# Merging two DMA transposes, moving four more chunks' transposes from PE to DMA, and splitting the last copy out of PSUM

## The chip, the cores and the metric

The kernel runs on one core of a Trainium2 chip. The core has five engines with an instruction stream each: PE (TensorE, matrix multiplication; its weight loads are shown as PEld), DVE (VectorE), ACT (ScalarE), POOL (GpSimd) and SP (SyncE, which here issues nearly all DMAs). Transfers run on 16 DMA engines beside them. The metric is the time of one execution in microseconds; the median of the runs of the kernel before is 185.22 us.

## What is computed

Two layers in a row, for 4 batches, 8 heads, 768 steps and a head size of 48. The first is a gated linear attention with a state per head, the second an MLP with a squared ReLU (the code calls it MoE) over 3072 tokens, with 384 inputs and 2048 hidden units:

```python
for t in range(S):
    state = alpha[:, :, t, :, None] * state + einsum('bhd,bhe->bhde', k[:, :, t], v[:, :, t])
    y[:, :, t] = einsum('bhd,bhde->bhe', q[:, :, t], state)
x = y.transpose(0, 2, 1, 3).reshape(B * S, H * D)
h = x @ w_in
out = (maximum(h, 0) ** 2) @ w_out
```

All inputs and the output are float32 in memory; the kernel multiplies in bf16.

## The kernel before

**Tiling.** Attention runs in chunks of 128 steps. There are 24 (variable `s`, 0 to 23), six for each of the four batches, and a chunk of attention makes exactly one tile of 128 tokens for the MLP. For a chunk, ACT takes the logarithm of alpha, PE sums it up over the steps with a triangular matrix, and ACT takes the exponential of the sums and of their negatives. q is multiplied by the one and k by the other on DVE. Their product over the head size (the PSUM tile `sc`) is masked on DVE (`sm`, line 566) and multiplied by v; the contribution of the state is added; ACT copies the result to bf16 (`xn`, line 615, through the helper of line 388).

**q and k with the head size on the partitions.** The product `sc` needs q and k transposed. For chunks below `RAW = 11`, PE transposes them after the multiplication. From chunk 11 on ("raw"), POOL casts q and k to bf16 (`rawb`, line 415) and SP issues a DMA transpose for each of them (line 418) from `rawb` into `rawt`. DVE then multiplies the transposed q (line 509) and k (`kz`, line 513, two instructions) by exponentials that were computed transposed. `rawb` and `rawt` have three buffers (`NR = 3`), so a cast waits for the transpose three chunks back, and a transpose for the multiplications three chunks back.

**x with the features on the partitions.** The MLP needs `xn` transposed as well (`xT_big`). For most chunks PE does it with three matmuls against an identity (`tr`, line 243), and DVE copies the result out of PSUM (line 633, recorded as line 390). For the chunks of `XTURN = (18, 23)`, that is 18 to 22, SP issues a DMA transpose instead (line 625).

**The MLP** runs over groups of token tiles, mostly pairs. The first matmul of a pair is 48 matmuls of 256 columns; ACT applies the ReLU (line 681), DVE squares (line 689); the second matmul is 16 matmuls of 384 columns a tile. A tile's result is copied from PSUM by ACT or DVE (lines 727 and 729) and stored by a DMA. A chunk's share of the two is about 5.1 us of PE.

**The order.** All instructions of an engine stand in an order that is fixed when the program is built. A planner (class `Plan`) makes it: it gives each operation an assumed duration and latency, goes through time, and on each engine picks the operation that can start first. A DMA transpose stands on the planner's own queue `TR`. It is taken to occupy the DMA engines for its duration, to be done at its start plus duration plus latency (`TLD` and `TLAT`), and to be issued `late` microseconds after it could be (`TLATE`), which moves it back in SP's list. PE is given a slack of 0.25 us behind other engines' results. On the chip nothing of these times remains, only the order: each engine runs its list and waits where an input is not there. SP runs its list in the same way, so an issue that waits holds the ones behind it.

**The gate.** A chunk's first matmul may be planned only when the MLP has come far enough. With `prog` the MLP work already picked, in microseconds:

```python
return s <= LEAD + (prog["m1"] + prog["m2"]) / 5.12
```

`LEAD` is 3.5, so attention runs at most 3.5 chunks ahead of the MLP's mean progress.

**The end.** From 163.7 us on only MLP work is left. The last tile's second matmul ends at 181.33 us; one ACT copy of 128x384, the DMA of the output and the program's closing follow.

Of the kernel before, what the change touches and what calls it, by code (L numbers as in the profile page):

```python
# [8 lines left out]
FP32 = mybir.dt.float32  # L9
# [45 lines left out]
def after(op, x=0.0):  # L55
    return (op, x)
# [85 lines left out]
def kernel(  # L142
# [10 lines left out]
    nc = tc.nc  # L153
    B, H, S, D = q.shape
    HD = H * D
    P = 128
# [3 lines left out]
    d_model, d_ff = moe_w_in.shape  # L160
# [3 lines left out]
    NT = n_tok // P  # L164
# [13 lines left out]
    opool = ctx.enter_context(tc.tile_pool(name="opool", bufs=6))  # L178
# [15 lines left out]
        out=utri_f, in_=utri_f, compare_op=ALU.is_ge, fill=0.0,  # L194
# [41 lines left out]
    def pin(ins):  # L236
        tc.keep_in_program_order(ins)
# [19 lines left out]
    X_SLACK = 0.2  # L257
    LD = 0.98
    LD1 = 1.0
    WLD = 2.1  # L260
    LAG = 3.2
    SQ_PRIO = 0.0

    def add(eng, dur, emit, *deps, **kw):
        return plan.add(Op(eng, dur, emit, deps, **kw))
# [41 lines left out]
    C = [dict() for _ in range(NT)]  # L307
# [58 lines left out]
    def add_load(s, nm):  # L366
        d = C[s]
        b, c = divmod(s, NCH)

        def ld():  # L370
            if nm not in d:
                d[nm] = loads.tile([P, H, D], FP32, name=nm)
            pin(nc.sync.dma_start(out=d[nm], in_=SRC[nm][b, c]))
        prev = C[s - LB].get("use_" + nm) if s >= LB else None
        d["ld_" + nm] = add("DMA", LD if s < 4 else LD1, ld, prev, lat=2.0 if s < 4 else LAG if s < 6 else 2.4, at=0.6)

    def add_chunk(s):
        d = C[s]
        b, c = divmod(s, NCH)
# [3 lines left out]
        g = dict(prio=-10.0 + s * 0.01)  # L383
# [26 lines left out]
        if raw:  # L410
            w, wz = s % NR, s % 2

            def e_rb(j, nm):
                raw_tiles()
                pin(nc.gpsimd.tensor_copy(R["b"][:, w, j, :, 0:D], d[nm]))  # L415

            def e_turn(j):
                pin(nc.sync.dma_start_transpose(out=R["t"][:, w, j], in_=R["b"][:, w, j].rearrange("p h d -> p (h d)")))
            rt = []
            for j, nm in enumerate(["qt", "kt"]):  # L420
                cb = add("POOL", 0.55, lambda j=j, nm=nm: e_rb(j, nm), d["ld_" + nm],
                         *([C[s - NR]["turn"][j]] if s >= RAW + NR else []), prio=-5.0)
# [57 lines left out]
        if raw:  # L480
# [8 lines left out]
            aT = add("ACT", 0.48, e_AT, pT, after(ai) if ai else None, **g)  # L489
            aiT = add("ACT", 0.48, e_AiT, pT, after(aT), *([C[s - 2]["p2"]] if s >= RAW + 2 else []), **g)  # L490
# [20 lines left out]
        def e_kz(hh):  # L511
            rows = slice(DP * hh, DP * hh + DP)
            pin(nc.vector.tensor_mul(R["z"][rows, wz, :, hh, :], R["t"][rows, w, 1], R["i"][rows, wz]))  # L513
        if raw:
            if not last:
                mk = d["use_kt"] = add("DVE", 0.47, e_kI, ai, d["ld_kt"], old, **g)
            cp = add("DVE", 0.34, e_qAT, aT, rt[0], **g)
            prz = C[s - 2]["p2"] if s >= RAW + 2 else None
            kz0 = add("DVE", 0.45, lambda: e_kz(0), aiT, rt[1], prz, **g)
            kz1 = add("DVE", 0.45, lambda: e_kz(1), aiT, rt[1], prz, after(kz0), **g)  # L520
# [50 lines left out]
        if not last:  # L571
# [7 lines left out]
            prev = C[s - 1].get("sb") if s else None  # L579
# [116 lines left out]
    def add_moe2(g, tt, before, box, quarters, pools):  # L696
# [22 lines left out]
        def e_ev():  # L719
# [7 lines left out]
                pin(nc.vector.tensor_copy(box["ob"], box["po"]))  # L727
            else:
                pin(nc.scalar.copy(box["ob"], box["po"]))  # L729
        ev = add({"DVE": 0.47, "ACT": 0.38}, 0, e_ev, op, prio=-15.0)  # L730
        box["first"].gives = ev

        def e_held():
# [11 lines left out]
        if pool_out:  # L745
            o = add("POOL", 1.0, e_out, ev, prio=5.0)
            o.late, o.moves = 0.5, 0.5
        else:
            add("OUT", 0.55, e_out, ev, at=0.0).late = OUT_LATE
        return op  # L750

    DMA_ORDER = ["at", (0, "qt"), (0, "kt"), (1, "qt"), (1, "kt"), (0, "vt"), (2, "qt"),
# [117 lines left out]
```

## Time and profile before

| | |
|---|---|
| median of 3 runs | 185.22 us (184.88 to 185.26) |
| the profiled execution | 186.47 us |
| its span, first to last instruction | 184.7 us |
| PE busy | 177.7 us (96%) |
| DVE, ACT, POOL busy | 130.6, 126.7, 41.8 us |
| matmuls for transposing `xn` (line 243) | 57, in 19 chunks |
| DMA transposes of q and k (line 418) | 26, landing after 2.6 / 3.3 / 5.2 us (min / median / max) |
| DMA transposes of `xn` (line 625) | 5, landing after 2.3 / 3.5 / 4.9 us |

The page gives the busy time of each engine, the same in 40 slices of the span (one digit is tenths), and the chain of work that ended last, followed back from the end. A row of a timeline has the start in us, the duration, engine, line, operation, written tile <- read tiles, and a count; brackets hold the idle time before it and what ended it. "SPq" is an issue by SP; "landing" is the time from an issue to its data's arrival. A DMA's issue on SP can contain a wait. Matmuls overlap: one with 256 columns is recorded as 272 ns, but they follow each other every 109 ns.

### The profile page before, as it was taken

To read this page: it belongs to the slowest core of one execution; us is meant where nothing else is said; L and a number is where in the kernel's file an instruction comes from. 1 tells how busy PE (TensorE), PEld (TensorE's weight loads), DVE (VectorE), ACT (ScalarE), POOL (GpSimd) and SP (SyncE) were. 2 spreads that over 40 slices of the span, in tenths; PEclk is the share of its full clock that TensorE was granted. 3 is DMA by queue.
4 is the path that set the end of the run, shared out by engine and by line. 5 is a ranking of instruction groups with operands and counts; after the bars stand their busy time and mean duration, and the time that the engine had idled before them with its cause. 6 is when DMAs were issued, how large, how long until landed. Compare 5 with 4: busy or idle time off the path is not lost.

```text
span 184.7 us, 4919 instructions
## 1 busy us (share of the span) xinstructions
PE 177.7 (96%) x1886; PEld 133.5 (72%) x1886; DVE 130.6 (71%) x283; ACT 126.7 (69%) x288; POOL 41.8 (23%) x81
## 2 busy tenths in 40 slices
PE   7798999999999999999999999999999999999992
PEld 2467795467868887977867867868876877978661
DVE  1248898965899998776878877868866786845100
ACT  3657699606867996958958958958965975848221
POOL 8121100011161134142224242243243311000000
PEclk9969999999999999999999999999999999999999
DMA  5999999999989888989999899999999967601112
GB/s 167 215 216 243 270 367 331 324 233 214 209 169 218 171 173 165 177 155 172 154 168 205 158 196 177 237 186 155 220 164 205 207 97 248 202 4 43 41 47 85
DMA packets 120056, 34.12 MB, mean 185 GB/s; under 512 B 112384, under 2 KB 118784, under 8 KB 120032
## 3 DMA queue, kind: packets, MB, share of 16 engines
q1 hardware_dynamic: 119392, 31.83, 83.6%
q0 software_dynamic: 640, 1.97, 3.1%
q8 instruction: 15, 0.25, 0.6%
q14 instruction: 9, 0.07, 0.2%
HBM read 25.17 MB, written 4.72 MB: 162 GB/s over the span
## 4 chain that ended last, share of the span: by engine, by line
PE 88%; ACT 6%; DMA 2%; issue 1%; DVE 1%; SPq 0%; ACTq 0%
PE bank L240 76%; PE sc L240 5%; PE bank L243 5%; ACT r L681 3%; DMA at<-in_alpha_dram 2%; PE st L240 2%; DVE w_out_b L295 1%; ACT A L464 0%; ACT gT L343 0%; ACT xn L388 0%; ACT Ainv L468 0%; ACT w_in_b L297 0%; ACT qkT L388 0%; ACT L_s L398 0%; ACT ob L729 0%
## 5 line engine op out<-in xcount | busy, mean ns | idle before, releaser
L240 PE MATMUL bank<-xT_big,w_in_b 128*128 128x256 bf16 (+2 forms) x636 | 73.6, 262 | 0.1
L240 PE MATMUL bank<-w_out_b,gT 128*128 128x384 bf16 x384 | 71.1, 326 | 0.5 <-DVE w_out_b L295 0.5
L681 ACT ACTIVATE r<-bank 128x512 bf16<-128x512 f32 x96 | 55.9, 618 | 7.3 <-PE bank L240 6.2
L240 PEld LDWEIGHTS <-w_in_b 128*128 128x128 bf16 x636 | 53.3, 98 | 8.0 <-issue 0.2
L240 PEld LDWEIGHTS <-gT 128*128 128x128 bf16 x400 | 36.0, 98 | 20.1 <-DVE w_out_b L295 1.0
L689 DVE TENSOR_TENSOR gT<-r 128x512 bf16<-128x512 bf16 x96 | 40.9, 455 | 9.6 <-ACT r L681 8.8
L566 DVE TENSOR_TENSOR sm<-sc,utri_b 128x512 bf16<-128x512 f32 x48 | 30.8, 684 | 5.9 <-PE sc L240 5.7
L407 POOL CAST vb<-vt 128x384 bf16<-128x384 f32 x24 | 13.5, 561 | 65.6 <-DMA vt<-in_v_dram 52.2
L729 ACT COPY ob<-bank 128x384 f32<-128x384 f32 x16 | 7.7, 478 | 19.1 <-PE bank L240 18.8
L507 DVE TENSOR_TENSOR kI_s<-kt,Ainv 128x384 bf16<-128x384 f32 x21 | 12.4, 591 | 7.3 <-ACT Ainv L468 7.3
L388 ACT CAST xn<-bank 128x384 bf16<-128x384 f32 x24 | 11.5, 479 | 8.3 <-PE bank L240 8.3
L415 POOL CAST rawb<-qt 128x384 bf16<-128x384 f32 x13 | 8.0, 614 | 19.8 <-DMA qt<-in_q_dram 15.7
L591 ACT CAST sb<-st 128x384 bf16<-128x384 f32 x20 | 9.7, 484 | 3.8 <-DVE st L586 3.6
L586 DVE TENSOR_TENSOR st<-st,ae_s 128x384 f32<-128x384 f32 x20 | 11.2, 559 | 1.5 <-ACT ob L729 0.5
L513 DVE TENSOR_TENSOR kz<-rawt,kz 64x512 bf16<-64x512 bf16 x26 | 11.5, 441 | 1.1 <-ACT kz L456 0.4
L415 POOL CAST rawb<-kt 128x384 bf16<-128x384 f32 x13 | 7.9, 607 | 17.7 <-DMA kt<-in_k_dram 16.5
L240 PE MATMUL bank<-warm 128*128 128x256 bf16 (+1 forms) x48 | 10.5, 356 | 1.3 <-DVE warm L188 1.3
L504 DVE TENSOR_TENSOR qA_s<-qt,A 128x384 bf16<-128x384 f32 x11 | 6.1, 551 | 7.7 <-ACT A L464 7.7
L398 ACT ACTIVATE L_s<-at 128x384 bf16<-128x384 f32 x20 | 10.6, 530 | 0.2
L468 ACT ACTIVATE Ainv<-bank 128x384 bf16<-128x384 f32 x21 | 10.6, 503 | 0.0
L240 PEld LDWEIGHTS <-qkT 64*128 64x128 bf16 (+1 forms) x168 | 7.9, 96 | 3.1 <-issue 0.8
L240 PEld LDWEIGHTS <-sm 128*128 128x128 bf16 x192 | 8.2, 96 | 1.5 <-DVE sm L566 0.2
(65 smaller groups left out, 181.4 us busy)
## 6 DMA issues: line engine op xcount, KB each, us to landing
qt<-in_q_dram SPq DMA_DIRECT2D x24, 192.0 KB, 4.1
kt<-in_k_dram SPq DMA_DIRECT2D x24, 192.0 KB, 3.7
vt<-in_v_dram SPq DMA_DIRECT2D x24, 192.0 KB, 3.8
at<-in_alpha_dram SPq DMA_DIRECT2D x20, 192.0 KB, 3.9
wo<-in_moe_w_out_dram SPq DMA_DIRECT2D x4, 768.0 KB, 8.3
out_dram<-ob POOLq DMA_DIRECT2D x10, 192.0 KB, 3.6
wi<-in_moe_w_in_dram SPq DMA_DIRECT2D x4, 384.0 KB, 5.4
wi<-in_moe_w_in_dram SPq DMA_DIRECT2D x2, 768.0 KB, 7.9
```

What stands on the lines that cost most here:

```text
L240: pin(nc.tensor.matmul(*a, **kw))
L388: pin(nc.scalar.copy(out_t, in_t))
L398: pin(nc.scalar.activation(L[:, :, 0:D], d["at"], AF.Ln))
L407: pin(nc.gpsimd.tensor_copy(d["vb"], d["vt"]))
L415: pin(nc.gpsimd.tensor_copy(R["b"][:, w, j, :, 0:D], d[nm]))
L468: pin(nc.scalar.activation(d["Ai"], d["pm"][:, 0:HD].rearrange("p (h d) -> p h d", h=H), AF.Exp, scale=-1.0))
L507: pin(nc.vector.tensor_mul(kI[:, :, 0:D], d["kt"], d["Ai"]))
L513: pin(nc.vector.tensor_mul(R["z"][rows, wz, :, hh, :], R["t"][rows, w, 1], R["i"][rows, wz]))
L566: pin(nc.vector.tensor_mul(d["sm"][:, hh], d["sc"][:, hh], utri_b.to_broadcast([P, NP, P])))
L586: pin(nc.vector.tensor_mul(st4, st4, bcast(ae, D)))
L681: pin(nc.scalar.activation(box["r"][:, 0:w], box["ph"][:, 0:w], AF.Relu))
L689: pin(nc.vector.tensor_mul(gT[g][:, f0:f0 + per, lo * P:lo * P + n], r, r))
```

## The change

Three edits and the planner's numbers that go with them.

1. For raw chunks, q and k of a chunk, which lie side by side in `rawb`, go through one DMA transpose of 128 x 1024 instead of two of 128 x 512. It waits for both casts. Both multiplications on DVE, and the cast three chunks later, now depend on that one transpose. The planner assumes 1.2 + 4.5 us with `late` 1.5 (before 1.0 + 4.0 and 2.0 for each of the two), and 0.93 instead of 1.0 us for each load from chunk 11 on.
2. `XTURN` becomes (14, 23): `xn` of chunks 14 to 17 is transposed by DMA too. The planner takes 0.6 + 9.5 us for it (`XLAT`; before 0.8 + 4.0) and issues it 0.2 instead of 1.0 us late. The gate lets attention lead by more: 0.25 chunk more for each chunk from 12 on, up to 1.25 from chunk 16 on.
3. The last token tile is copied from PSUM by DVE (columns 0 to 191) and ACT (192 to 383); the planner may start both together, and the output's DMA waits for both.

```diff
+    LD2 = 0.93
...
-    XTURN = (18, 23)
-    TLD, TLAT, TLATE = 1.0, 4.0, 2.0
+    XTURN, XLAT = (14, 23), 9.5
+    TLD, TLAT, TLATE = 1.2, 4.5, 1.5
...
-        d["ld_" + nm] = add("DMA", LD if s < 4 else LD1, ld, prev, lat=2.0 if s < 4 else LAG if s < 6 else 2.4, at=0.6)
+        d["ld_" + nm] = add("DMA", LD if s < 4 else LD1 if s < RAW else LD2, ld, prev, lat=2.0 if s < 4 else LAG if s < 6 else 2.4, at=0.6)
...
-            def e_turn(j):
-                pin(nc.sync.dma_start_transpose(out=R["t"][:, w, j], in_=R["b"][:, w, j].rearrange("p h d -> p (h d)")))
+            def e_turn():
+                pin(nc.sync.dma_start_transpose(
+                    out=R["t"][:, w].rearrange("p j n t -> p (j n) t"), in_=R["b"][:, w].rearrange("p j h d -> p (j h d)")))
...
-                t_ = add("TR", TLD, lambda j=j: e_turn(j), cb, *([C[s - NR]["turned"][j]] if s >= RAW + NR else []), lat=TLAT)
-                t_.late = TLATE
-                rt.append(t_)
-            d["turn"] = rt
+                rt.append(cb)
+            d["turn"] = turn = add("TR", TLD, e_turn, *rt, *(C[s - NR]["turned"] if s >= RAW + NR else []), lat=TLAT)
+            turn.late = TLATE
...
-            d["x"] = add("TR", 0.8, e_xt, xn, lat=TLAT)
-            d["x"].late = 1.0
+            d["x"] = add("TR", 0.6, e_xt, xn, lat=XLAT)
+            d["x"].late = 0.2
...
+        def e_half(eng, lo, hi):
+            if eng == "DVE":
+                box["ob"] = opool.tile([P, d_model], FP32, name="ob")
+                pin(nc.vector.tensor_copy(box["ob"][:, lo:hi], box["po"][:, lo:hi]))
+            else:
+                pin(nc.scalar.copy(box["ob"][:, lo:hi], box["po"][:, lo:hi]))
+        half = None
+        if t == NT - 1:
+            half = add("DVE", 0.26, lambda: e_half("DVE", 0, d_model // 2), op, prio=-15.0)
+            ev = add("ACT", 0.22, lambda: e_half("ACT", d_model // 2, d_model), op, after(half, -9.0), prio=-15.0)
+        else:
+            ev = add({"DVE": 0.47, "ACT": 0.38}, 0, e_ev, op, prio=-15.0)
...
-            return s <= LEAD + (prog["m1"] + prog["m2"]) / 5.12
+            return s <= LEAD + min(1.25, max(0.0, 0.25 * (s - 11))) + (prog["m1"] + prog["m2"]) / 5.12
```

More of the change, by code (lines that the diff above doesn't have):

```diff
@@ L421, in add_chunk @@
                 cb = add("POOL", 0.55, lambda j=j, nm=nm: e_rb(j, nm), d["ld_" + nm],
-                         *([C[s - NR]["turn"][j]] if s >= RAW + NR else []), prio=-5.0)
+                         C[s - NR]["turn"] if s >= RAW + NR else None, prio=-5.0)
                 d["use_" + nm] = cb
-                t_ = add("TR", TLD, lambda j=j: e_turn(j), cb, *([C[s - NR]["turned"][j]] if s >= RAW + NR else []), lat=TLAT)
-                t_.late = TLATE
-                rt.append(t_)
-            d["turn"] = rt
+                rt.append(cb)
+            d["turn"] = turn = add("TR", TLD, e_turn, *rt, *(C[s - NR]["turned"] if s >= RAW + NR else []), lat=TLAT)
+            turn.late = TLATE
         vb = d["use_vt"] = add("POOL", 0.55, e_vb, d["ld_vt"], old, prio=-5.0)
@@ L516, in add_chunk @@
                 mk = d["use_kt"] = add("DVE", 0.47, e_kI, ai, d["ld_kt"], old, **g)
-            cp = add("DVE", 0.34, e_qAT, aT, rt[0], **g)
+            cp = add("DVE", 0.34, e_qAT, aT, turn, **g)
             prz = C[s - 2]["p2"] if s >= RAW + 2 else None
-            kz0 = add("DVE", 0.45, lambda: e_kz(0), aiT, rt[1], prz, **g)
-            kz1 = add("DVE", 0.45, lambda: e_kz(1), aiT, rt[1], prz, after(kz0), **g)
+            kz0 = add("DVE", 0.45, lambda: e_kz(0), aiT, turn, prz, **g)
+            kz1 = add("DVE", 0.45, lambda: e_kz(1), aiT, turn, prz, after(kz0), **g)
             d["turned"] = [cp, kz1]
@@ L729, in e_ev @@
                 pin(nc.scalar.copy(box["ob"], box["po"]))
-        ev = add({"DVE": 0.47, "ACT": 0.38}, 0, e_ev, op, prio=-15.0)
+        def e_half(eng, lo, hi):
[10 more added lines that the diff above has]
+            ev = add({"DVE": 0.47, "ACT": 0.38}, 0, e_ev, op, prio=-15.0)
         box["first"].gives = ev
@@ L748, in add_moe2 @@
         else:
-            add("OUT", 0.55, e_out, ev, at=0.0).late = OUT_LATE
+            add("OUT", 0.55, e_out, ev, half, at=0.0).late = OUT_LATE
         return op
```

## The prediction

> **What bounds the kernel now.** I read the page from its top: busy shares and slices, then the chain that ended last, then that chain over stretches, and last the rows of what the change touches. The page:
>
> ```profile
> PE 177.7 (96%) x1886; PEld 133.5 (72%) x1886; DVE 130.6 (71%) x283; ACT 126.7 (69%) x288; POOL 41.8 (23%) x81
> ...
> PE   7798999999999999999999999999999999999992
> ...
> DMA  5999999999989888989999899999999967601112
> ...
> PE 88%; ACT 6%; DMA 2%; issue 1%; DVE 1%; SPq 0%; ACTq 0%
> ```
>
> PE is busy in every slice but the first and the last, and 88% of the chain lies on it. The reader should see a second full row: the DMA engines are near full until slice 31 (145 us). The windows put numbers on both; the columns are PE, PEld, DVE, ACT and POOL busy, the clock, the DMA share and GB/s:
>
> ```profile
> 100.00:120.00 20.00, 20.00 (x219) 16.42 (x218) 16.64 (x37) 16.30 (x39) 6.32 (x11) 1.00 1.07 194
> 120.00:140.00 20.00, 20.00 (x198) 14.96 (x197) 15.60 (x33) 15.13 (x37) 6.98 (x12) 1.00 1.04 188
> 140.00:160.00 20.00, 19.95 (x213) 15.87 (x212) 14.43 (x31) 14.46 (x34) 4.37 (x8) 1.00 0.88 192
> ```
>
> PE has no hole at full clock, so in this stage only fewer matmuls shorten the kernel, and any input that comes late lengthens it one for one. The waits of PE agree: five in all, 3.3 us, and the chain has the last of them at 34 us. The chain at the end:
>
> ```profile
> 163.56 0.17 PE bank L243 x3
> 163.73 17.60 PE bank L240 x124
> 181.33 0.02 issue
> 181.35 0.48 ACT ob L729
> ```
>
> The first line is the price of one chunk's transposes of x on PE, the last the copy that the third edit splits.
>
> **The change part by part.** *x by DMA for chunks 14 to 17.* Four chunks lose their three matmuls of line 243. At 0.17 us each, on a gapless PE, that is 4 x 0.17 = 0.68 us off the end. Their four DVE copies (xT_big L390, 350 ns each) go too; DVE is 72 to 83% busy in these windows and PE doesn't wait for it, so this gives nothing.
>
> In exchange SP gets four more DMA issues. For x an issue takes 1207 ns at least and 1352 in the median, and lands after 2.3 to 4.9 us. The planner books 0.6 + 9.5, with its slack of 0.25 makes 10.35 us, from the end of xn to the first use; for chunk 19 it books 5.05 now, and the trace has xn ending at 138.02 and the use at 143.09, so that order carries over to the chip. The landing is thus 5 us ahead of its user. To fill the 10.35 us, PE must have other work: the gate lets later chunks start 0.25 chunk earlier per chunk, up to 1.25 x 5.12 = 6.4 us from chunk 16 on, and two tiles of the second matmul (2.6 us each, 16 x 163 ns) can go ahead, as one did before 143.09. Taken at nothing; uncovered, it would cost up to 4.9 us.
>
> SP is in order, so a transpose of x that waits for xn holds the loads and transposes queued behind it. The three issued among the loads, at 130.31, 138.04 and 143.95, had gaps of at most 0.43 us in front. Being placed 0.8 us earlier (late 1.0 becomes 0.2), each could hold SP 1.2 us; kept as an end.
>
> *The earlier chunks need q and k earlier.* This is the step that can hurt. The 26 transposes L418 are two a chunk from chunk 11 on; their use is the multiplication kz. For chunks 15, 16 and 17:
>
> ```profile
> 96.64 1.20 SPq L418 DMA_TRANSPOSE rawt<-rawb  x1
> ...
> 102.98 1.21 SPq L418 DMA_TRANSPOSE rawt<-rawb  x1
> ...
> 109.58 1.20 SPq L418 DMA_TRANSPOSE rawt<-rawb  x1
> ```
> ```profile
> 105.70 1.14 DVE L513 TENSOR_TENSOR kz<-rawt,kz 64x512 bf16<-64x512 bf16 x2
> ...
> 112.56 1.02 DVE L513 TENSOR_TENSOR kz<-rawt,kz 64x512 bf16<-64x512 bf16 x2
> ...
> 119.15 0.86 DVE L513 TENSOR_TENSOR kz<-rawt,kz 64x512 bf16<-64x512 bf16 x2
> ```
>
> With the median landing of 3.3 us the slack is 5.8, 6.3 and 6.3 us. The lead takes 5.1, 6.4 and 6.4 of it: 0.7, -0.1 and -0.1 are left if nothing arrives earlier. So the lead spends what slack there is, and the sign hangs on the merged transpose.
>
> *One transpose for q and k.* Thirteen of the 26 issues go. An issue takes 1189 ns at least and 1269 in the median, and the 384-column form (x, 1207) is no cheaper than the 512-column one, so I take 1.3 us for the 1024-column one; the other end is two old ones, 2.5. Added up over the SP rows from 80 to 147 us, 21 transposes of q and k, 3 of x and 37 loads fill 62 of 67 us, 12 us of it above the shortest issue of each kind. By chunk 17, seven issues saved (8.9 us) stand against three of x (4.1 us): inputs can come some 4 us earlier, which is the slack I count on. The bytes don't shrink: by the packet records a transpose of 512 columns is 512 packets of 18 ns on 16 engines, 0.58 us, two of them 1.15; four loads are 4 x 0.96; x adds 0.43. That is 5.0 a chunk, 5.4 with x and 5.9 with an output, against a chunk every 6.7 us now (the spacing of kz above) and 5.4 while the lead grows. q now also waits for the cast of k, 1 to 2 us later; on SP the next loads queue behind that wait, but the second of the two old issues made it already. DVE uses q only 1 us ahead of k (104.72 and 105.70), so k set the time already. POOL's casts wait for the transpose three chunks back, some 20 us old: nothing. Cost in the sum: nothing, with bounds of 0 and of a PE wait of 1.9 us (worked out below).
>
> *The last tile in two halves.* DVE copies columns 0 to 191, ACT the rest, of the same PSUM tile. ACT's full copy takes 478 ns (384 columns); against the 843 ns of its 768-column row that is 0.95 ns a column, so a half is 0.30. DVE's full copy takes 558 (keep L727), and sm (512 columns) 684: 0.98 a column, a half 0.37. Side by side the copy ends after 0.37 instead of 0.48: 0.11 gained. One after the other with a 0.05 hand-over: 0.37 + 0.05 + 0.30 = 0.72, 0.24 lost. Nothing covers it: the output's issue, landing and closing follow. The trace has no two readers of one tile; the nearest row is PE writing one half of a tile while ACT reads the other:
>
> ```profile
> 15.75 0.10 PEld L243 LDWEIGHTS <-kI_s 128*128 128x128 bf16 x1
> 15.83 0.58 ACT L388 COPY qkT<-bank 128x512 bf16<-128x512 bf16 x1 [0.35 <-PE bank L243]
> ...
> 16.47 0.33 PE L243 MATMUL bank<-ident_bf,kI_s 128*128 128x128 bf16 x3 [0.51 <-ACT qkT L388]
> ```
>
> The weights were in at 15.85, and still the matmul waited for ACT, though it touches other columns. Two engines on one tile are made to take turns here, so I take 0.24 lost. The Trainium skill speaks against the edit too: PSUM — Partial Sum Buffer, section PSUM bank collisions raise a hardware error, says that ACT and DVE must not touch one bank in the same partitions at once, not even to read different columns, and that software has to order them. No run here shows two readers; by that rule the halves come one after the other, and without it the sum below would be 0.35 us lower.
>
> **The sum.** -0.68 + 0.24 = -0.44 us. The profiled execution took 186.47 us, 184.7 of span and 1.77 around it, which becomes 186.03. It lies 1.25 above the median of the runs, so I take the difference over: 185.22 - 0.44 = 184.78.
>
> **The rivals.**
> *Halves side by side*: -0.68 - 0.11 = -0.79, 184.43. For it: DVE and ACT are both idle at 181.3 and start within tens of ns of a signal. Against it: the row at 16.47.
>
> *PE waits for q and k (the slower side).* Place: the sc matmul of chunks 16 to 22, after kz; DVE is in order too, so the squares L689 queue behind a late multiplication and with them the second matmul. If the DMA engines are full, as 1.04 to 1.07 says, the merged issue buys nothing and the transposes of x push the loads back by 4 x 0.43 = 1.7 us; with the 0.1 to 0.2 us of missing slack PE waits up to 1.9 us, once, since all later chunks shift with it. It decides from 0.44 + 0.37 = 0.81 us of wait on. Middle of 0.81 and 1.9: 1.35, which gives 186.1. Were the merged issue 2.5 us, three x issues (4.1 us) would make it worse still; the equal issue times speak against that. Against the rival: 5.4 to 5.9 us of packets in 6.7 us leaves the engines some room.
>
> *The gain drowns in small waits.* PE lost 1 us in small pieces between 50 and 60 us and 0.3 between 140 and 150, beyond each matmul's usual pace; a new order can cost 0.1 to 0.8 us elsewhere. Middle 0.45: 185.2.
>
> **How the numbers follow.** A measurement can tell about 0.2% here, 0.37 us: 184.85 to 185.59 is no change. My forecast, 184.78 (own range 184.5 to 185.1), gets 0.50, of which 0.32 lies below 184.85; halves side by side 0.16, all faster; small waits 0.15, of which 0.11 no change and 0.04 slower; late q and k 0.19, slower, about half of it above 186.2. Faster 0.48, same 0.18 + 0.11 = 0.29, slower 0.23. The range runs from 184.3, below the side-by-side case, to 186.2, inside the late case; some 0.15 is left out.
>
> **What the profile after will show.** Line 243 on xn 45 times instead of 57, and L625 nine times; right if PE is gapless from 60 to 180 us. L418 13 times, issue near 1.3 us: the step on SP's relief. The kz of chunks 16 to 22 some 6 us earlier against the matmuls around them, their transposes landed before; a wait of PE on kz means the late rival. At the end a DVE and an ACT row of 128x192: starts 0.4 us apart confirm the turn-taking, together refute it. The forecast is wrong if PE shows waits over 0.8 us after 60 us, or if the plan itself leaves PE without work ahead of the group of chunks 14 and 15.

## The result and the profile after

| | before | after |
|---|---|---|
| median of 6 executions | 185.18 us (184.83 to 185.28) | 187.25 us (186.30 to 190.35) |
| ratio, 95% interval | | 1.011 (1.0072 to 1.0148) |
| the profiled execution, its span | 186.47, 184.7 us | 187.08, 185.4 us |
| PE busy | 177.7 us | 176.3 us |
| start of the MLP group of chunks 8 and 9 to the end of PE's work | 108.66 us | 110.03 us |
| landing of the last output to the end of the span | 0.96 us | 1.52 us |

The kernel became 1.1% slower, outside the predicted range. In three later comparisons, told below, the same kernel came out at 1.0065, 1.0138 and 1.0024, so the size of the loss is itself a finding. The profiled execution of before reached the first matmul of the MLP group of chunks 8 and 9 at 72.65 us, that of after at 71.21, so stretches are compared from that matmul on. Some executions of a kernel come out several us longer than the rest: the ratios leave them out, and as the profiled executions of e12, e13 and e16 are such, nothing rests on e12's and e13's alone, and e16's, at a granted clock of 0.66, is not read. In the kernel after, lines up to the copy's are one higher: the transposes on PE are still line 243, the transposes of q and k are line 419, those of x 626, the logarithm of alpha 399, kz 514. The halves are lines 734 (DVE) and 736 (ACT).

The page after, busy times, PE's slices and the chain by engine:

```profile
PE 176.3 (95%) x1873; PEld 132.4 (71%) x1874; DVE 131.2 (71%) x283; ACT 125.2 (68%) x285; POOL 40.4 (22%) x81
...
PE   7898999999999999999999999699999999999991
...
PE 71%; DMA 9%; ACT 9%; DVE 5%; issue 3%; SPq 2%; POOL 1%; POOLq 0%; DVEq 0%; ACTq 0%
```

PE has 1.4 us less to do, and a hole that was not there: the 6 in the 26th slice, at about 118 us. The chain lies on PE for 71% instead of 88%; DMA (9% instead of 2), DVE (5 instead of 1) and ACT (9 instead of 6) have most of what PE lost. The windows (columns as before: PE, PEld, DVE, ACT, POOL, clock, DMA share, GB/s) give the hole its size:

```profile
100.00:120.00 20.00, 18.55 (x184) 13.47 (x182) 13.41 (x28) 13.11 (x32) 6.26 (x12) 1.00 0.97 196
120.00:140.00 20.00, 19.83 (x206) 15.71 (x204) 16.93 (x38) 17.08 (x43) 5.92 (x11) 1.00 1.03 196
```

1.45 us of PE are missing in the first, 0.17 in the second; before, both were 20.00. The chain that ended last says through what the loss came, and shows the new end:

```profile
113.11 1.07 SPq L374
114.19 0.05 issue
114.24 3.62 DMA at<-in_alpha_dram
117.88 0.52 ACT L_s L399
118.41 0.49 ACT qkT L454
118.89 0.37 ACT ob L730
119.26 0.50 ACT kz L457
119.76 0.49 ACT r L682
120.30 0.82 PE bank L240 x6
...
157.70 23.56 PE bank L240 x170
181.28 0.37 DVE ob L734
181.67 0.32 ACT ob L736
```

From the top: SP issues the load of alpha for chunk 21 at 114.24, it lands at 117.86, ACT takes its logarithm (L_s), then does four other things, and one of these lets PE go on. PE's own timeline:

```profile
116.77 1.25 PE L240 MATMUL bank<-xT_big,w_in_b 128*128 128x256 bf16 x10
119.31 0.82 PE L240 MATMUL bank<-xT_big,w_in_b 128*128 128x256 bf16 x6 [1.29 <-ACT ob L730]
120.30 0.82 PE L240 MATMUL bank<-xT_big,w_in_b 128*128 128x256 bf16 x6 [0.17 <-ACT ae_s L461]
```

The matmul at 119.31 belongs to the MLP and has nothing to do with alpha. It waits for ACT's copy `ob` out of PSUM, and that copy stands in ACT's list behind a logarithm for a chunk whose `kz` comes 22 us later. How the logarithm got there is seen from chunk 21's load and logarithm, before and after. Before, SP's and ACT's timelines:

```profile
117.81 1.17 SPq L373 DMA_DIRECT2D at<-in_alpha_dram  x1
...
125.74 0.52 ACT L398 ACTIVATE L_s<-at 128x384 bf16<-128x384 f32 x1
```

And after:

```profile
114.24 0.64 SPq L374 DMA_DIRECT2D at<-in_alpha_dram  x1
...
117.88 0.52 ACT L399 ACTIVATE L_s<-at 128x384 bf16<-128x384 f32 x1 [1.95 <-DMA at<-in_alpha_dram]
```

The logarithm moved 7.9 us to the front, its load only 3.6 (the later start of before's execution is 1.4 of either). Before, alpha was there 4.0 us early; after, ACT stood idle for 1.95 us until it landed. PE's wait of 1.29 us is over the 0.8 us that the prediction had named as a sign of being wrong. The planner had booked for SP's work: loads at 0.93 instead of 1.0 us, one transpose at 1.2 instead of two at 1.0, x at 0.6. Between 80 and 147 us SP had issues for 62 of 67 us, as before: 18.8 us for 11 merged transposes, 31.3 for 36 loads, and 11.8 instead of 4.0 for x.

### The profile page after: what moved, and what is told of

Its sections match the earlier page's. It is cut to its first block, busy times and chain, and to the rows that moved or that the text cites. A ratio compares the mean times of both kernels' runs of the same rounds, so it can differ in the third digit from the quotient of the medians.

```text
span 185.4 us, 4861 instructions
## 1 busy us (share of the span) xinstructions
PE 176.3 (95%) x1873; PEld 132.4 (71%) x1874; DVE 131.2 (71%) x283; ACT 125.2 (68%) x285; POOL 40.4 (22%) x81
## 4 chain that ended last, share of the span: by engine, by line
PE 71%; DMA 9%; ACT 9%; DVE 5%; issue 3%; SPq 2%; POOL 1%; POOLq 0%; DVEq 0%; ACTq 0%
PE bank L240 62%; DMA qt<-in_q_dram 4%; DMA at<-in_alpha_dram 4%; PE bank L243 4%; PE sc L240 4%; ACT r L682 4%; PE st L240 1%; SPq L374 1%; DVE sm L567 1%; DVE gT L690 1%; SPq L419 1%; ACT xn L389 1%; POOL rawb L416 1%; ACT L_s L399 1%; DVE w_out_b L296 1%
## 5 line engine op out<-in xcount | busy, mean ns | idle before, releaser
L240 PE MATMUL bank<-xT_big,w_in_b 128*128 128x256 bf16 (+2 forms) x635 | 74.6, 262 | 1.8 <-ACT ob L730 1.3
L240 PE MATMUL bank<-w_out_b,gT 128*128 128x384 bf16 x384 | 70.2, 326 | 0.5 <-DVE w_out_b L296 0.5
L730 ACT COPY ob<-bank 128x384 f32<-128x384 f32 x14 | 6.8, 483 | 13.9 <-PE bank L240 13.8
L508 DVE TENSOR_TENSOR kI_s<-kt,Ainv 128x384 bf16<-128x384 f32 x21 | 12.9, 612 | 2.3 <-ACT Ainv L469 2.3
L505 DVE TENSOR_TENSOR qA_s<-qt,A 128x384 bf16<-128x384 f32 x11 | 6.8, 620 | 7.6 <-ACT A L465 7.6
L416 POOL CAST rawb<-qt 128x384 bf16<-128x384 f32 x13 | 7.1, 543 | 22.1 <-DMA qt<-in_q_dram 22.1
L240 PE MATMUL bank<-vb,sm 128*128 128x48 bf16 x192 | 9.1, 184 | 0.0
```

What stands on the lines that cost most here:

```text
L240: pin(nc.tensor.matmul(*a, **kw))
L508: pin(nc.vector.tensor_mul(kI[:, :, 0:D], d["kt"], d["Ai"]))
```

## The experiments

Every ratio is to the kernel before on the same chip, with its 95% interval. "PE part" is the stretch from the first matmul of the group of chunks 8 and 9 to the end of PE's work in the one profiled execution: 108.66 us before, 110.03 after. "Slack" is the time from the landing of a chunk's transposed q and k to the multiplication `kz` that needs them.

### One part at a time

**e1: before, with the last tile in halves alone.** The edit is the third part of the change in the kernel before:

```diff
+        if t == NT - 1:
+            half = add("DVE", 0.26, lambda: e_half("DVE", 0, d_model // 2), op, prio=-15.0)
+            ev = add("ACT", 0.22, lambda: e_half("ACT", d_model // 2, d_model), op, after(half, -9.0), prio=-15.0)
```

> The kernel before with the last tile's two halves alone. The traces of before and after put the end of the last matmul to the issue of the output at 0.52 us with one ACT copy (181.33 to 181.86) and at 0.74 us with the halves one after the other (181.28 to 182.02). Turn-taking theory: 0.2 us slower than before, 185.4. Rival (the halves cost nothing, the rest of the tail hides them): 185.2. Nothing else changes in the order.

185.56 us, ratio 1.0020 (0.9995 to 1.0044). From PE's end to the output's issue it takes 0.77 us, before 0.54. The timeline of the kernel after shows why:

```profile
180.75 0.49 PE L240 MATMUL bank<-w_out_b,gT 128*128 128x384 bf16 x2
181.28 0.36 DVE L734 COPY ob<-bank 128x192 f32<-128x192 f32 x1 [11.95 <-PE bank L240]
181.67 0.32 ACT L736 COPY ob<-bank 128x192 f32<-128x192 f32 x1 [2.51 <-DVE ob L734]
```

ACT starts 35 ns after DVE ends, and what it waits for is DVE's copy (the bracket): the halves are ordered by a semaphore in the program as built, although the planner may start them together, and they cost 0.23 us at the end.

**e2 and e14: after, with the last tile in one ACT copy.** The same kernel in two comparisons:

```diff
-        if t == NT - 1:
+        if False:
```

> The changed kernel with the last tile copied by ACT in one piece. If the halves are 0.2 us of the loss: 187.0, still over 1.5 us slower than before, with PE waiting for about 2 us between 95 and 125 us. Rival: most of the loss is in the tail, then 185.5.

> The changed kernel with the last tile in one piece, beside the changed kernel. If the halves cost what the traces show, 0.23 us: 0.12% under the changed kernel, that is still 0.4% or more over the kernel before, and as widely spread. If the piece copy really is level with the kernel before, the halves do more than their 0.23 us.

185.44 us, 1.0005 (0.9984 to 1.0026), and 186.50 us, 1.0016 (0.9983 to 1.0049). PE parts 108.11 and 108.37 us: 0.3 to 0.55 below before's, where 0.68 was predicted. In e2 alpha of chunk 21 landed just as ACT got to its logarithm, and nothing waited; in e14 ACT waited 0.31 us and PE did not. So e2's time is that of the rival, but not for its reason: the end explains 0.23 us, and the wait for alpha was simply absent.

**e3: the merged transpose alone**, with its numbers in the planner; x from chunk 18 and the gate as before, no halves. Against the kernel after:

```diff
-    XTURN, XLAT = (14, 23), 9.5
+    XTURN, XLAT = (18, 23), 4.0
...
-            d["x"] = add("TR", 0.6, e_xt, xn, lat=XLAT)
-            d["x"].late = 0.2
+            d["x"] = add("TR", 0.8, e_xt, xn, lat=XLAT)
+            d["x"].late = 1.0
...
-            return s <= LEAD + min(1.25, max(0.0, 0.25 * (s - 11))) + (prog["m1"] + prog["m2"]) / 5.12
+            return s <= LEAD + (prog["m1"] + prog["m2"]) / 5.12
```

> One transpose for q and k with the new booked times, x by DMA from chunk 18 on as before, no extra lead, no halves. Theory A (the loss comes from asking for the inputs 6 us earlier while x goes through the same queue): the merged transpose alone is harmless, 185.0 to 185.3, PE without waits over 0.3 us after 60 us. Rival C (the merged transpose is itself slow and holds SP's list, so inputs come late without any lead): over 185.8, PE waits on inputs of chunks 15 to 22.

185.78 us, 1.0034 (1.0005 to 1.0062), a little over the 185.0 to 185.3 of theory A. The merge does what it says: q and k of chunks 14 to 23 now land 10 to 16 us ahead of `kz` (before 5 to 8), and q of chunk 17 is loaded from 92.5 on instead of 101.4. PE has no new gap (PE part 108.44). That it is none the less a shade slower fits the closing: 1.29 us instead of 0.96 from the landing of the output to the end. It books the same times as the change for the loads and for q and k, so those alone do not make the inputs late.

**e4: x by DMA and the lead alone**, with two transposes as before, no halves. Against the kernel after:

```diff
-    LD2 = 0.93
+    LD2 = 1.0
...
-    TLD, TLAT, TLATE = 1.2, 4.5, 1.5
+    TLD, TLAT, TLATE = 1.0, 4.0, 2.0
...
-            def e_turn():
+            def e_turn(j):
...
-        if t == NT - 1:
+        if False:
```

> x by DMA from chunk 14 on with the lead and the 9.5 us, but two transposes of q and k with the times booked before, no halves. Theory A: the four chunks' transposes save 0.68 us, and the inputs cannot be there 6 us earlier; PE loses 0.8 us or more: 185.3 to 187. Rival C (only the merged transpose does harm): 184.5.

189.81 us, 1.0245 (1.0204 to 1.0286), PE part 112.57, a larger loss than theory A had. What PE waited for, by the waits (us in total, times, longest):

```profile
PE sc L240 <- DVE kz L514: 1.8, 4, 0.8
...
PE st L240 <- POOL vb L408: 1.0, 2, 0.8
```

This is the prediction's slower rival, late q and k, in the kernel where nothing relieves SP: the slack is 0.0 to 0.1 us in chunks 14, 16 to 19 and 21, so what SP can't issue in time PE waits for, v too (`vb`). With the merged transposes the slack in the kernel after is 1.6 to 7.3 us: q and k are not late there.

### The logarithm of alpha

**e5 and e18: the kernel after again**, on two more chips, and **e13** on a third; no edit.

> The changed kernel as it is, beside the next three on one chip. The piece copy without halves came out level with the kernel before on another chip (185.44 against 185.39), so either the loss of 2 us belongs to the halves (then about 187.2 here too) or it comes and goes with the timing of the loads (then 185.4 to 186.5 here, with single executions of 188 and more, and a profile in which PE's wait near 118 us is shorter or absent).

> The changed kernel once more, for the three beside it: 0.6 to 1.1% over the kernel before, as measured so far, with executions spread over 2 us or more.

> The changed kernel once more, beside the two above on one chip: 1.0065 to 1.0138 by its three measurements so far. If it comes at or under 1.003 here, the size of the loss is a matter of the chip and the run, and the halves have no part in it.

1.0065 (1.0035 to 1.0094), 1.0138 (1.0096 to 1.0180) and 1.0024 (1.0006 to 1.0042); medians 186.49, 188.47 and 185.69 us. ACT's row for chunk 21 in e13 and then in e18:

```profile
120.40 0.52 ACT L399 ACTIVATE L_s<-at 128x384 bf16<-128x384 f32 x1 [2.78 <-DMA at<-in_alpha_dram]
```
```profile
117.86 0.52 ACT L399 ACTIVATE L_s<-at 128x384 bf16<-128x384 f32 x1
```

In e18 alpha had landed 1.4 us before, and nothing waited. The table sets all kernels with these lists of SP and ACT (but for the last copy) side by side, by how late alpha came:

| | alpha(21) landed, from the start of the group of chunks 8 and 9 | ACT waited | PE waited for `ob` | PE part |
|---|---|---|---|---|
| e13 | 47.4 | 2.78 | 2.1 | 112.37 |
| after | 46.7 | 1.95 | 1.3 | 110.03 |
| e5 | 45.8 | 1.15 | 0.5 | 109.26 |
| e17 (below) | 45.8 | 0.99 | 0.3 | 109.13 |
| e14 | 45.0 | 0.31 | 0 | 108.37 |
| e2 | 44.8 | 0 | 0 | 108.11 |
| e18 | 43.5 | 0 | 0 | 108.45 |

Of every wait of ACT, PE gets all but 0.7 us, and the PE part grows with it (e13 lost another 1.2 us to `sc` from 143.5 us on). So the kernel stands on an edge: alpha lands within 4 us from one execution to another, ACT waits from some 45 us on, and PE from 0.7 us later. A profile is one execution; the ratios, over many, follow the same order but for e18, whose ratio is 1.0024.

**e6: the logarithm later in ACT's list**, by letting the planner believe that alpha lands 8 us later. SP's list is the same instruction for instruction; those of ACT, DVE and PE are rearranged in other places too, since the planner works through them anew:

```diff
-        d["ld_" + nm] = add("DMA", LD if s < 4 else LD1 if s < RAW else LD2, ld, prev, lat=2.0 if s < 4 else LAG if s < 6 else 2.4, at=0.6)
+        d["ld_" + nm] = add("DMA", LD if s < 4 else LD1 if s < RAW else LD2, ld, prev, lat=2.0 if s < 4 else LAG if s < 6 else 2.4 + (8.0 if nm == 'at' and s >= 14 else 0.0), at=0.6)
```

> The changed kernel, but from chunk 14 on the planner takes alpha to land 8 us later, so that the logarithm stands later in ACT's list (for chunk 21 by 4 us); SP's list is the same. Theory L (ACT is held by a logarithm whose alpha is late, and the ReLUs behind it starve PE): the waits of ACT on alpha go, PE's wait near 118 us goes, 184.9 to 185.2 and little scatter, that is 0.7 us under the changed kernel or more. Rival S (q and k or x are late too): no faster than the changed kernel.

185.39 us, 1.0015 (0.9990 to 1.0040), where the kernel after stood at 1.0065 on the same chip. The intervals overlap a little. The group of the logarithm on the page of the kernel after (busy and mean ns, then idle time before it):

```profile
L399 ACT ACTIVATE L_s<-at 128x384 bf16<-128x384 f32 x20 | 10.5, 526 | 3.1 <-DMA at<-in_alpha_dram 3.0
```

and on that of e6, with its window:

```profile
L399 ACT ACTIVATE L_s<-at 128x384 bf16<-128x384 f32 x20 | 10.5, 523 | 0.1
```
```profile
100.00:120.00 20.00, 19.90 (x204) 15.06 (x204) 15.69 (x34) 15.04 (x38) 5.79 (x11) 1.00 1.01 205
```

Chunk 21's logarithm stands at 119.53 now, 3.8 us behind alpha's landing. ACT waits for alpha no more, PE gets 19.90 of 20 us, and the PE part is 108.05. By itself this execution decides nothing: its alpha landed at 44.7 us on the scale of the table, where e2 did not wait either. The execution of e9 below does, which has the same lists of ACT and PE. There alpha landed at 46.2, between e5 and after, and the logarithm came 2.1 us behind it without a wait:

```profile
120.70 0.54 ACT L399 ACTIVATE L_s<-at 128x384 bf16<-128x384 f32 x1
```

e9's PE part is 108.02, and PE never waits for `ob` in it.

**e7: the loads of alpha off SP's list**, issued by POOL from chunk 14 on; the logarithm where the change put it:

```diff
-            pin(nc.sync.dma_start(out=d[nm], in_=SRC[nm][b, c]))
+            pin((nc.gpsimd if nm == "at" and s >= 14 else nc.sync).dma_start(out=d[nm], in_=SRC[nm][b, c]))
```

> The changed kernel with alpha's loads from chunk 14 on issued by POOL, so that ten issues of 0.6 to 2.1 us leave SP's list; the bytes stay. If SP's list is what makes inputs late: q and k of chunks 17 to 22 are issued 4 us and more earlier than in the changed kernel, alpha lands before its logarithm, 185.0. If the DMA engines are full: q and k land within 1 us of where they land in the changed kernel. If POOL's issues hold its casts, the transposes come later and it is slower than the changed kernel.

185.58 us, 1.0017 (0.9993 to 1.0041), PE part 107.90. This is the cleanest edit: the lists of ACT, DVE and PE are those of the kernel after. Alpha of chunk 21 landed 0.7 us ahead of its logarithm, and PE did not wait. Two rows of SP's timeline, the transpose of q and k of chunk 17 and that of x of chunk 15, show how far SP lags. In the kernel after:

```profile
104.66 1.52 SPq L419 DMA_TRANSPOSE rawt<-rawb  x1
...
109.46 1.30 SPq L626 DMA_TRANSPOSE xT_big<-xn  x1
```

In e7:

```profile
101.17 1.67 SPq L419 DMA_TRANSPOSE rawt<-rawb  x1
...
106.29 1.59 SPq L626 DMA_TRANSPOSE xT_big<-xn  x1
```

x of chunk 15 was ready at 106.2 in the kernel after, and SP got to it 3.3 us later; in e7 it goes at once. One such row proves little, since in e18, with the unchanged list, x of chunk 15 goes at once too. But for chunks 17 to 20 SP is 4.3 to 6.8 us behind `xn` in the kernel after and 3.6 to 6.7 in e18, and only 1.2 to 2.2 in e7. The bytes on the DMA engines are the same, which speaks for SP's list and not the engines as what runs late.

**e12: the loads of alpha one chunk earlier in SP's list**, the logarithm left in place:

```diff
-                if nm == "at" and 9 <= d < NT - 1:
-                    add_load(d + 1, nm)
+                if nm == "at" and d == 12:
+                    add_load(13, nm)
+                if nm == "at" and 9 <= d < NT - (2 if d >= 12 else 1):
+                    add_load(d + (2 if d >= 12 else 1), nm)
```

> The changed kernel with alpha's loads issued one chunk earlier from chunk 14 on, and the logarithms in their places. If ACT's wait for a late alpha is the cause: alpha lands 3 us or more ahead of its logarithm from chunk 14 to 22, PE has no wait over 0.4 us near 118 us, and the time is as with the later logarithm, 0.1 to 0.2% over the kernel before. If not: 0.6% and more over it, as the changed kernel beside it.

188.22 us, 1.0086 (1.0043 to 1.0129), so the time did not come down to the expected 0.1 to 0.2%. Alpha landed 5 to 12 us ahead of its logarithm in chunks 14 to 21 (0.7 in chunk 22), and the wait at 118 us was gone. Another was there:

```profile
140.83 0.23 PE L240 MATMUL sc<-qkT,kz 128*128 128x128 bf16 x1 [1.02 <-DVE kz L514]
141.57 0.56 PE L240 MATMUL sc<-qkT,kz 128*128 128x128 bf16 x7 [0.51 <-DVE kz L514]
```

q and k of chunk 21 had 0.4 us of slack left. That the earlier loads of alpha made them late is not shown: in e13, on the same chip, with the list of the kernel after, they had 1.1 us left, and PE waited 1.2 us at the same matmul.

### The lead, and the halves once more

**e8: less lead and less time for x.**

```diff
-    XTURN, XLAT = (14, 23), 9.5
+    XTURN, XLAT = (14, 23), 6.0
...
-            return s <= LEAD + min(1.25, max(0.0, 0.25 * (s - 11))) + (prog["m1"] + prog["m2"]) / 5.12
+            return s <= LEAD + min(0.5, max(0.0, 0.25 * (s - 11))) + (prog["m1"] + prog["m2"]) / 5.12
```

> The changed kernel with 6.0 instead of 9.5 us booked for x and a lead of at most 0.5 instead of 1.25 chunks, so that inputs are wanted 3.8 us later. Theory of the lead (it spent the slack): multiplications kz of chunks 16 to 22 start 6 us or more after their transposes landed, alpha is 2 us or more ahead of its logarithm, PE gapless: 184.9 to 185.1 with the halves still in. Rival (x then comes late, since its transposes were issued 3 to 6 us after xn in the changed kernel): PE waits for x ahead of the groups of chunks 14 to 21, over 185.8.

188.03 us, 1.0138 (1.0100 to 1.0176), PE part 110.59. PE's waits, with the time from the timeline:

```profile
115.07 1.48 PE L240 MATMUL bank<-xT_big,w_in_b 128*128 128x256 bf16 x12 [1.05 <-DMA xT_big<-xn]
```
```profile
128.96 1.47 PE L240 MATMUL bank<-xT_big,w_in_b 128*128 128x256 bf16 x12 [1.42 <-DMA xT_big<-xn]
```

The slack of q and k is 6 to 14 us from chunk 14 on, but x of chunk 15 is issued 3.3 us after `xn`, lands at 115.0 and PE has been waiting for it. So the inputs have time again and x has not: the rival held. The edit cuts the lead and the time booked for x together, so it does not say which of the two had covered x.

**e16 and e17: both halves on ACT (`e_half` then copies on ACT throughout), and the whole last tile on DVE**, beside e18 on one chip:

```diff
-            half = add("DVE", 0.26, lambda: e_half("DVE", 0, d_model // 2), op, prio=-15.0)
+            half = add("ACT", 0.22, lambda: e_half("ACT", 0, d_model // 2), op, prio=-15.0)
```
```diff
         if t == NT - 1:
+            ev = add("DVE", 0.47, e_ev, op, prio=-15.0)
+        elif False:
             half = add("DVE", 0.26, lambda: e_half("DVE", 0, d_model // 2), op, prio=-15.0)
```

> The changed kernel with both halves of the last tile copied by ACT, one after the other; DVE's list ends as without halves. What is open: the changed kernel came out at 1.0065 to 1.0138 of the kernel before, without its halves at 1.0005 and 1.0016, although the halves by themselves cost 0.2 us. Theory that the halves cost only what the end of the trace shows: two ACT copies of about 0.31 us in place of one of 0.48, so 0.15 us above the kernel without halves, ratio 1.002, and the rest of the spread is by how late alpha comes. Rival, that the DVE instruction added at the end of the program is what disturbs: 1.001 to 1.003 here as well, but the changed kernel above 1.006. Rival, that any second instruction there (ACT's list as long as with halves) disturbs: above 1.006 here too.

> The changed kernel with its last tile copied whole by DVE (ACT's list one instruction shorter, DVE's as long as in the changed kernel). The end costs 0.56 us of copy in place of ACT's 0.48, so 0.1 us above the kernel without halves: 1.001 to 1.003 where only the end's cost counts. Rival, that the DVE instruction at the end of the program disturbs what is far ahead of it: above 1.006, with alpha of chunk 21 landing 46 us or more after the first matmul of chunk 8's MLP group against 45 without halves.

185.31 us, 1.0008 (0.9987 to 1.0029), and 185.62 us, 1.0025 (1.0006 to 1.0045), with the kernel after at 1.0024. On this chip no form of the last copy differs measurably from another. The added instruction is neither needed for the wait nor enough for it: e14, without it, waits 0.31 us for alpha, and e18, with it, has the earliest alpha of the table. On the chip of e13 and e14, where the kernel after was 1.2% above the one without halves, of which the halves explain 0.23 us, the rest stays unexplained; the profile of e13 shows it as a later SP list, not why it is later.

### The closing

**e9: after, without halves, the logarithm late, and four small loads more on SP.** They go into a tile that nobody uses, behind the output of tile 20, and shift what follows in SP's list:

```diff
+            if t == 20:
+                fill = consts.tile([P, 64], FP32, name="fill")
+                for i in range(4):
+                    pin(nc.sync.dma_start(out=fill[0:16, 16 * i:16 * i + 16], in_=moe_w_out[0:16, 16 * i:16 * i + 16]))
```

> The later logarithm of the run before, the last tile in one piece, and four small loads (16 x 16 elements, their data unused) that SP issues after the output of tile 20, where it stands idle. In the changed kernel SP's closing holds 0.39 us between its two drains that the kernel before has not, in each of the four runs with the same SP list. If that belongs to where the closing lies in SP's instruction list, four more instructions move it: 0.05 us between the drains, landing of the output to the end 1.0 to 1.2 us instead of 1.5, and the time 0.5 us under the kernel before (PE's 0.68 us, less some scatter): 184.8. If it belongs to something else, the gap of 0.39 stays and the time is 185.1. Single executions over 186.5 should be as rare as with the kernel before.

185.42 us, 1.0009 (0.9982 to 1.0035), neither the 184.8 nor the 185.1 expected. In the kernel after SP's last instructions hold a gap of 0.385 us (184.118 to 184.503) that before has not, but that e2, e5, e8, e13 and e14 have too, all with as many SP instructions. With four instructions more the gap of 0.38 us lies four instructions earlier (183.081 to 183.461), and the closing takes 1.71 us instead of 1.5. In all kernels that show it, the gap is ahead of the 208th recorded instruction of SP (they have 211 to 215); e3, with 206, e7, e11 and e15, with 195, have none, and in e10, with 213, that place falls into the wait for the last landing. The gap thus sits at a fixed place in SP's list, and whether it falls behind the last landing goes with the list's length. In the DMA view of the kernel after, from 180 us on, there is a transfer that before has not there:

```profile
q14 instruction: 1, 0.01, 0.5%
```

Queue 14 is labelled as instructions; before, its last transfer is at 160.5 us. But SP does not stand because it waits for this transfer: it starts at 185.13 us, 0.6 us after the gap has ended, in e9 as well (184.09, gap to 183.461), and e3 has such a transfer at 184.54 without a gap. What the stop is stays open.

### What beats both

**e10: x by DMA from chunk 12 on**, no halves, the logarithm late from chunk 12 on, the lead from one chunk earlier; **e11**, the same with the loads of alpha on POOL from chunk 12 on, and **e15**, e11 once more. Against the kernel after, e10, and then e11 against e10:

```diff
-    XTURN, XLAT = (14, 23), 9.5
+    XTURN, XLAT = (12, 23), 9.5
...
-        if t == NT - 1:
+        if False:
...
-            return s <= LEAD + min(1.25, max(0.0, 0.25 * (s - 11))) + (prog["m1"] + prog["m2"]) / 5.12
+            return s <= LEAD + min(1.25, max(0.0, 0.25 * (s - 10))) + (prog["m1"] + prog["m2"]) / 5.12
```
```diff
-            pin(nc.sync.dma_start(out=d[nm], in_=SRC[nm][b, c]))
+            pin((nc.gpsimd if nm == "at" and s >= 12 else nc.sync).dma_start(out=d[nm], in_=SRC[nm][b, c]))
```

> x by DMA from chunk 12 on, the lead growing from chunk 11 on, the later logarithm from chunk 12 on, the last tile in one piece. PE loses two more chunks' transposes, 0.33 us: 1.0 us less PE work than before, 184.3 to 184.7 if the inputs still come. Rival (the two more issues and the earlier lead overload SP's list while the lead grows): the multiplications kz of chunks 12 to 17 wait for their transposes, PE waits on sc, 185.3 or more.

> As the run before, and alpha's loads from chunk 12 on issued by POOL. If SP's list is the limit, x is issued within 1 us after xn and q and k land 3 us and more earlier than in the run before, so that PE has no wait over 0.3 us after 75 us: 184.3 to 184.6. If the DMA engines are the limit, landings are as in the run before and so is the time.

> The fastest kernel so far once more (x by DMA from chunk 12 on, later logarithm, alpha's loads from POOL, last tile in one piece): 0.3 to 0.8% under the kernel before.

184.73 us, 0.9992 (0.9956 to 1.0028); 184.26 us, 0.9947 (0.9918 to 0.9977); 184.94 us, 0.9943 (0.9913 to 0.9973) on a chip where before took 185.89. The version with POOL beats both kernels, the one before by 0.55%. It saves six chunks' transposes on PE, 6 x 0.17 = 1.0 us; the PE part is 107.46 in e11's profile, where PE has no wait over 0.3 us after 75 us, as expected, and the closing is 1.16 in both. In e15's profile PE waits again, 1.2 us for `kz` and 0.4 for x (PE part 109.27), so this kernel stands near the same edge. e10 has the same lists of ACT, DVE and PE, and stays at before's time within its interval. That the room on SP makes the difference is not shown: the intervals of e10 and e11 overlap, and in e10's profile PE waits for only 0.2 us after 75 us (PE part 107.79).

## Why the prediction was wrong, step by step

**x off PE, -0.68 us: right.** The rows of line 243 and line 626 after:

```profile
L243 PE MATMUL bank<-ident_bf,xn x45: 219/219/229, 14.1 to 157.5; 128*128 128x128 bf16 x45
...
L626 SPq DMA_TRANSPOSE xT_big<-xn x9: 1180/1399/1917, 102.1 to 150.8; - x9
```

45 and nine, as said, and wherever nothing waited for alpha the PE part is 0.2 to 0.8 us shorter than before's 108.66 (e18, e2, e6, e7); e1, with the same work as before, has 108.79.

**One transpose at 1.3 us: right.** Its shortest issue is 1.242 us, against 1.189 for half the columns; the median of 1.571 holds waits. It lands after 3.7 us in the median, before 3.3:

```profile
L419 SPq DMA_TRANSPOSE rawt<-rawb x13: 1242/1571/2325, 69.6 to 141.7; - x13
```

**The landing of x, "taken at nothing": right as it stood.** In the kernel after PE never waits for x. e8 shows that this hangs on the lead and the time booked for x: with less of both PE waits 2.5 us in two places.

**The halves, 0.24 us lost: right**, 0.23 measured, 35 ns apart. The rule of the Trainium skill that was weighed there, PSUM — Partial Sum Buffer, section PSUM bank collisions raise a hardware error, agrees with these rows; the rival of halves side by side falls. What orders the two here is a semaphore; no run shows what they would do without it.

**"The earlier chunks need q and k earlier": this is the step that failed, by what it left out.** It took the slack of one input, q and k, and set the lead of up to 6.4 us against it. The lead brings forward everything that a chunk does ahead of `kz`, the logarithm of alpha too, whose slack before was smaller: between landing and logarithm 2.4, 5.0, 2.5, 5.1, 3.4, 2.8 and 4.0 us in chunks 15 to 21, where q and k had 5.5 to 8.0. The same subtraction (5.1 us of lead in chunk 15, 6.4 behind) would have left -3.9 to -1.3 us, ahead of any relief of SP. "Cost in the sum: nothing" rested on the one input; what the runs show in its place is a wait of ACT for alpha of 1.95 us, of which PE lost 1.46 (1.29 and 0.17). In size that is within the 1.9 us that the prediction allowed for late q and k, but it came by another way. I looked at `kz` because it is the last step ahead of `sc`, and took the chain's edge of late inputs to lie there; but an engine that takes its list in order stands at the first input that is missing, however little hurry its user is in. ACT did not need this logarithm then: in e6 and e9 it comes 3.4 to 3.7 us later after the first matmul of chunks 8 and 9 than in e18, and nobody waits.

**The relief of SP, "some 4 us earlier, which is the slack I count on": right where it was counted, wrong behind it.** The sum was made up to chunk 17, with seven issues saved against three of x. q of chunk 17 is indeed loaded at 94.9 instead of 101.4. But each further chunk adds a transpose of x, and the lead stays: q of chunks 20 and 21 is loaded at 117.8 and 123.9, before at 119.0 and 126.1, which is the offset of 1.4 us between the two executions and little more. Alpha of 21 is in the same list. e4 shows the same from the other side: without the merge, q and k are late.

**The rivals.** Late q and k, given 0.19 and 186.1 us, has the sign and half the size, but not the place: that rival is what e4 does, and, in addition to alpha, e13's execution at chunk 21. In the kernel after it is alpha, ACT and a PSUM copy that queue up. The Trainium skill says in PSUM — Partial Sum Buffer, section Engine vs sequencer instructions, that ScalarE takes its queue strictly first in, first out; the rows at 117.88 and behind agree, where four steps whose inputs were there stand behind the wait of 1.95 us.

**A term that was missing: the closing.** "The output's issue, landing and closing follow" was taken as unchanged. It takes 0.96 us before and in e1, and 1.48 to 1.52 in every kernel with the list of SP that the kernel after has: 0.53 us, of which the stop is 0.38.

**The sum by the runs.** Without the wait: -0.6 (PE part of e6, 108.05 - 108.66) + 0.23 (halves) + 0.53 (closing) - 0.1 (1.70 instead of 1.80 us around the span) = +0.06 us; e6 and e7 measured 0.28 and 0.31 above before, with intervals that reach from -0.2 to 0.8. The sum is from single executions and good to half a microsecond or so: with e7's PE part and closing it gives -0.45. So even without alpha the change brought no gain that these runs can show. The wait adds 0 to 1.5 us to that in the executions read (2.3 in e13's); with the halves and the closing this accounts for most of the loss, but not for all of it: for the profiled execution of after it gives some 1.5 us, where the median is 2.1 above that of before.

## What to carry to other kernels

Who moves a step ahead must take the time off the slack of every input of every instruction that moves with it, on each engine, not only of the one that the edit touches; the smallest slack decides, and an in-order engine passes the wait on to work that has nothing to do with it. A planner that is told shorter issue times than the chip takes may build an order that the queue can't follow; that was not tested by itself here, and e3, with the same times booked for the loads and for q and k, had no late input. The fastest kernel here has independent loads on a second queue (POOL), though how much of its gain comes from that is not shown. Where a result differs from comparison to comparison, look for a race between two lists and order the executions by it.

## What was new about the hardware

- A DMA transpose costs SP nearly the same for twice the columns: 1.19 us at least for 512, 1.24 for 1024, where many plain loads take 0.53 to 0.58; its landing went from 3.3 to 3.7 us in the median.
- SP's closing has a stop of 0.36 to 0.39 us ahead of its 208th recorded instruction, and so it comes and goes with the list's length: 0.92 to 1.71 us from the landing of the output to the end over these kernels. What it is stays open; the transfer on the instruction queue starts 0.6 us after it.
- Two copies by DVE and ACT of different columns of one PSUM tile, ordered by a semaphore, follow each other 35 ns apart (after, e1).
- In the same program alpha of chunk 21 landed 43.5 to 46.7 us behind the same matmul (47.4 in e13's execution), and on one chip (e17, e18, which differ in the last copy alone) 2.2 us apart. What makes SP's list run earlier or later was not found.
